# Attention and a low-rank mixer on one core: another order of the opening, up to batch 0's mixing

## The chip, the cores and the metric

The kernel runs on one core of a Trainium2 chip. A core has a matrix engine (TensorE, PE in the profile, with its weight loads as PEld), a vector engine (VectorE, DVE), a scalar engine (ScalarE, ACT), a general engine (GpSimd, POOL) and SyncE (SP), which only issues transfers. Each engine takes its instructions in order from its own queue and waits on semaphores for the others. Transfers between device memory and the on-chip memory (SBUF) are issued from SP's, ACT's or POOL's queue; those that change the type from float32 to float16 on the way are issued from POOL's. Matrix products are written to PSUM, which has eight banks here, and other engines read them from there.

The metric is the device time of one execution in microseconds (us), as a median over runs. The profile is of one execution on the same core.

## The reference

For 8 batches, 8 heads, 576 tokens and head size 64, it computes causal attention in which 16 extra "beacon" keys and values stand ahead of the batch's own, then a mixer on the attention's output `x` of 8 x 576 x 512:

```python
k_all = np.concatenate([beacon_k, k], axis=2)          # 16 + 576 keys
v_all = np.concatenate([beacon_v, v], axis=2)
scores = scale * np.matmul(q, k_all.transpose(0, 1, 3, 2))
scores = np.where(causal, -1000000000.0, scores)
a = softmax(scores)                                    # over the keys
x = np.matmul(a, v_all)                                # heads side by side: 512 columns
h = x.transpose(0, 2, 1) @ U @ V                       # U: 576 x 32, V: 32 x 576, along the tokens
u = x + h.transpose(0, 2, 1)
out = u + np.maximum(u @ w_ch1, 0.0) @ w_ch2           # 512 -> 2048 -> 512
```

## The kernel before

The work of the attention is cut into pairs of heads: pair `p` is heads `2c` and `2c+1` of batch `b`, with `b, c = divmod(p, 4)`, so pairs 0 to 3 are batch 0. For each pair q and k are brought into a tile `pr` (regroup, L240) and, for batch 0, a small head tile is cast beside it (L565). They are turned on PE (`qkT_units`, L248 and L250, into PSUM `tps`) and copied out as `qT` and `kT` (L251, L252; by ACT at L511). Scores are products at L304 into `sps`; one exponential per group of columns goes from there to `expt` (L310, ACT); the causal mask is a minimum with `bigmask`, which holds four blocks of the triangular `mask`, and with one small block of `mask` (L291, L293, DVE). The weighted sum of one head is 15 products at L328 into `po`; a column of ones in `vs` gives the divisor, and DVE divides (L336, L337) into `xb`.

When a batch has its eight heads in `xb`, it is mixed (`mix_units`): `head` multiplies with U (L368) and copies the result to `qts` (L374); two `part`s bring `xb` into `ups` by products with the identity (L387), add V times `qts` (L394), and copy to `uT` (L403 on DVE, L405 on ACT). V is spread over four groups of 32 partitions by a product with a selector `sel`, four identities side by side (`spread`, L157, copied at L160).

`uT` is then read by the two-layer network in blocks of 512 tokens (`mlp_units`). A block has 16 units of the hidden layer, dc 0 to 15, of four products each (L428, `gps`), each followed by a maximum with zero (L432, L434); then come units of the second layer (L445) and the output. w1 is loaded in four quarters of 512 columns by `emit_w1(i)` (L167): quarter `i` is what dc `4i` to `4i+3` read. w2 comes in two halves (`emit_w2`, L172).

The order of everything is written out by hand in `SCRIPT`, a string of steps. Under `tc.manual_schedule` each engine's queue has its instructions in the order in which the steps emit them. The steps that matter here:

- `GqV0`: regroup q of pair 0 on DVE (V; A is ACT, G is POOL). `TkA1`: turn k of pair 1, copied out by ACT.
- `Sa0:2`, `Sb0`: scores and exponentials of pair 0, groups 0 and 1, or 2 and 3; the number after the colon is how many idle products go first. `M0`: its masks. `A0.1`: the weighted sum of its second head.
- `I3`: three idle products of identity and identity, 512 columns each (`keep_warm`, L228), whose result is not used.
- `X0.0`, `X0.1`, `X0.2`: batch 0's mixing, head and two parts. After `X0.2` block 0's units join a list, and a step that is a number takes so many units from it; ahead of that the list is empty, and a number does nothing.
- `k1A`, `q1B`, `b1`, `v1A`: loads of batch 1, heads 0 to 3 (A) or 4 to 7 (B), by POOL; `b1` is its beacon keys. `w10` to `w13`, `w20`, `w21`: the quarters of w1 and the halves of w2, by POOL too.
- `u`: the small loads of U and V by SP (L141 to L146); `cV`: their casts (L150, L151); `eV`: the spread of V.

Batch 0's q and k are loaded as float32 by SP and ACT, ahead of the script. POOL's queue carries all the loads named above, and an issue there also waits until an earlier one of the same queue has landed: eight semaphores are used in turn (`semaphore=111` to `118` in the trace).

Of the kernel before, what the change touches and what calls it, by code (L numbers as in the profile page):

```python
# [17 lines left out]
P = 128  # L18
F16_MAX = 65504.0
# [8 lines left out]
def kernel(  # L28
# [75 lines left out]
    def pst(shape, dtype, name):  # L104
        return psum.tile(shape, dtype, tag="ps", name=name)


    ident = const.tile([P, P], F16, name="ident", tag="ident")
    make_identity(nc, ident)
    mask = const.tile([P, P], F16, name="mask", tag="mask")  # L110
    make_upper_triangular(nc, mask, val=F16_MAX, diag=True)
    bigmask = const.tile([P, 4, P], F16, name="bigmask", tag="bigmask")
    nc.vector.tensor_copy(out=bigmask[:, 0, 0 : P - Nb], in_=mask[:, Nb:P])
    nc.vector.memset(bigmask[:, 0, P - Nb : P], F16_MAX)
    for c in range(1, 4):
# [16 lines left out]
    def small_loads():  # L132

        f = utp.tile([P, NT * R + S], F32, name="small", tag="ut")
        uf, vf = f[:, 0 : NT * R].rearrange("p (j r) -> p j r", r=R), f[0:R, NT * R :]
        one = utp.tile([R, P + S], F16, name="one", tag="ut")
        sel, Vone = one[:, 0:P], one[:, P:]
        for cc in range(NCC):
            nc.vector.tensor_copy(out=sel[:, ts(cc, R)], in_=ident[0:R, 0:R])
        nc.vector.memset(uf[0:Nb, 0, :], 0.0)  # L140
        nc.sync.dma_start(out=uf[Nb:P, 0, :], in_=moe_U[0 : nq[0], :])  # L141
        nc.sync.dma_start(
            out=uf[:, 1 : NT - 1, :], in_=moe_U[q0[1] : QM, :].rearrange("(j p) r -> p j r", p=P)
        )
        nc.sync.dma_start(out=uf[:NL, NT - 1, :], in_=moe_U[QM:S, :])
        nc.sync.dma_start(out=vf, in_=moe_V)  # L146

        def cast(copy):
            for rr, jj in ((P, slice(0, NT - 1)), (NL, slice(NT - 1, NT))):
                copy(out=Usb[:rr, jj, :], in_=uf[:rr, jj, :])  # L150
            copy(out=Vone, in_=vf)  # L151
# [12 lines left out]
    def emit_w1(i):  # L164
        w1r = moe_w_ch1.rearrange("(cc p) f -> p cc f", p=P)
# [57 lines left out]
    def keep_warm(ps, n):  # L223


        w = ps.shape[-1] // P
        for _ in range(n):
            nc.tensor.matmul(  # L228
                ps[:, 0 : w * P].rearrange("p (a b) -> p a b", b=P), ident,
                ident.rearrange("p (a b) -> p a b", a=1).broadcast_to([P, w, P]),  # L230
                start=True, stop=True,
            )
# [386 lines left out]
    late = {}  # L619

    def step(t):
        name, arg = t[0], t[1:]
        if t.isdigit():
            fill(int(t))
        elif name == "I":
            keep_warm(pst([P, 512], F32, name="idle"), int(arg))
        elif name in "kqbv":
            b, hs = int(arg[0]), HALVES[arg[1:]]
            if name == "k":
                k_loads(b, L_of(b), hs)  # L630
# [36 lines left out]
        M2 A2.0 GqA5 A2.1 M3 GqA4 1 A3.0 w12 v1A A3.1 GkA5 eV w20 TqA5 GkA4 X0.0 1 X0.1 X0.2 TkA5 TqA4 TkA4 2  # L667
        k1B w21 2 v1B GqV6 Sb5 1 GqA7 Sa4 1 q2 2 Sb4 2 M4 4 A4.0 Sa5:0 2 GkA6 GkV7 M5 1 TqV6 1 A5.1 TkA6 b3
        A5.0 k2 1 A4.1 TkA7 Sa6:0 1 Sb6 TqV7 GqV8 2 GqV9 Sa7 2 M6 Sb7 b2 1 v2 A6.1 GkV9 GkV8 M7 1 TqV8 2 GkV10
        1 A6.0 GqA10 TqA10 q3 1 A7.1 A7.0 2 X1.0 X1.1 X1.2 TkA10 TqV9 TkV9 1 TkA8 1 Sa9 Sa8 3 Sb8 1 k3 GqA11 1  # L670
        v3 Sb9 M8 2 A8.1 A8.0 1 GkV12 1 GqV12 Sa10 1 M9 GkV11 R12 Sb10 1 M10 1 TkV11 1 A10.0 TqA11 4 GkA13
        A9.1 A9.0 Sa11 1 TkV12 GqV15 Sb11 1 k4 A10.1 2 GkA14 GqV13 1 TqA12 b5 Sa12 1 GqA14 M11 R13 R14 3 GkA15
        Sb12 1 A11.0 1 M12 A11.1 q4 TkA13 b4 TkV14 TqA13 Sa13 R15 A12.0 TqV14 1 TqV15 1 GkA16 3 Sb13 v4 1
        A12.1 M13 X2.0 2 Sb14 GqA18 A13.0 X2.1 TkV15 X2.2 A13.1 Sa14 k5 q5 GkA17 Sb15 GqA17 GqA16 R16 R17 1
# [134 lines left out]
```

## Time and profile before

| | us |
|---|---|
| median of 3 runs | 362.17 |
| lowest and highest of them | 361.27, 363.23 |
| the profiled execution, its own time | 360.71 |
| its span | 359.0 |
| busy in it: PE, ACT, DVE, POOL | 346.4, 207.0, 189.4, 82.8 |

A row of the timeline gives the start, the duration, the engine, the line, the operation, what it writes and reads, how many instructions are merged in it, and in brackets how long the engine had been idle and what ended that. "q" behind an engine's name means its queue, which issues a transfer; the time of an issue is not that of the transfer. A row of a stretch gives its length and then, per engine, busy time with the number of instructions, at its end PE's granted clock (1.00 is full speed), the share of the transfer engines and GB/s.

### The profile page before, as it was taken

The page shows a single profiled execution, that of the slowest core. Times are in us where ns is not written, and L with a number is a line of the kernel's source. Part 1 is how long each engine was busy: PE and PEld are TensorE (multiplying, and loading weights), DVE is VectorE, ACT ScalarE, POOL GpSimd, SP SyncE. Part 2 cuts the span into 40 slices and gives each one's busy share as a digit, 9 for nine tenths or more (in the row PEclk, how much of TensorE's full clock was granted, in tenths as well). Part 3 has the DMA queues.
Part 4 walks back from the last instruction along what each step waited for, and adds up shares of the span by engine and source line. Part 5 has one row for each costly group of instructions (what it writes and reads, how often), then busy time and mean ns, then how long its engine had stood idle before and what let it go on. Part 6 is the DMA issues. An engine that isn't in the chain of part 4 may idle for free.

```text
span 359.0 us, 7688 instructions
## 1 busy us (share of the span) xinstructions
PE 346.4 (96%) x3018; PEld 176.9 (49%) x3018; DVE 189.4 (53%) x528; ACT 207.0 (58%) x438; POOL 82.8 (23%) x119
## 2 busy tenths in 40 slices
PE   5989999999998999999999999999999999999995
PEld 2455478844545435454444544454544544444443
DVE  3884355546649455574757436774564446313311
ACT  3997866398579878658644954679335302401400
POOL 5993648601309006300620050000000000000000
PEclk9898999999999999999999999999999999999999
DMA  7999999992959969995999694663323123112111
GB/s 199 158 172 195 180 192 170 203 157 43 165 127 123 162 123 119 181 218 106 94 171 201 132 93 108 126 107 66 88 85 70 20 77 89 30 58 85 36 55 69
DMA packets 134396, 43.57 MB, mean 121 GB/s; under 512 B 106545, under 2 KB 130353, under 8 KB 134353
## 3 DMA queue, kind: packets, MB, share of 16 engines
q0 software_dynamic: 69008, 17.54, 51.4%
q1 hardware_dynamic: 64896, 25.17, 34.2%
q8 instruction: 25, 0.41, 0.5%
q10 hardware_dynamic: 448, 0.30, 0.3%
q14 instruction: 19, 0.15, 0.1%
HBM read 37.63 MB, written 9.44 MB: 131 GB/s over the span
## 4 chain that ended last, share of the span: by engine, by line
PE 86%; ACT 4%; DMA 4%; DVE 2%; POOL 1%; issue 1%; SPq 1%; ACTq 0%
PE cps L445 35%; PE gps L428 32%; PE po L328 7%; PE sps L304 7%; ACT expt L310 2%; DMA raw<-pr 2%; DMA vs<-in_v_dram 2%; PE ups L387 1%; PE ups L394 1%; PE tps L250 1%; POOL vs L190 1%; DMA stm<-in_k_dram 1%; PE qtp L368 1%; ACT pr L511 1%; ACT qT L511 1%
## 5 line engine op out<-in xcount | busy, mean ns | idle before, releaser
L310 ACT ACTIVATE expt<-sps 128x496 f16<-128x496 f32 (+2 forms) x256 | 110.7, 543 | 41.4 <-PE sps L304 38.6
L445 PE MATMUL cps<-w,gT 128*128 128x512 f16 (+1 forms) x656 | 134.2, 353 | 0.0
L428 PE MATMUL gps<-uT,w 128*128 128x512 f16 x576 | 132.8, 379 | 0.3 <-DVE xb L337 0.2
L432 ACT ACTIVATE gT<-gps 128x512 f16<-128x512 f32 x86 | 51.9, 621 | 70.0 <-PE gps L428 69.3
L445 PEld LDWEIGHTS <-gT 128*128 128x128 f16 x656 | 60.5, 98 | 57.6 <-issue 4.4
L428 PEld LDWEIGHTS <-w 128*128 128x128 f16 x576 | 53.0, 98 | 64.3 <-issue 3.5
L434 DVE TENSOR_SCALAR gT<-gps 128x512 f16<-128x512 f32 x58 | 39.9, 689 | 50.0 <-PE gps L428 48.0
L458 DVE TENSOR_TENSOR ob<-cps,ut 128x512 f32<-128x512 f32 (+1 forms) x33 | 22.2, 674 | 47.0 <-PE cps L445 46.6
L190 POOL DMA_DIRECT2D vs<-in_v_dram x50 | 40.7, 822 | 11.2 <-DMA w<-in_moe_w_ch_dram 5.6
L328 PEld LDWEIGHTS <-expt 128*128 128x128 f16 (+1 forms) x960 | 35.2, 98 | 13.8 <-DVE expt L291 2.2
L328 PE MATMUL po<-vs,expt 128*128 128x65 f16 (+1 forms) x960 | 38.4, 194 | 2.1 <-DVE expt L291 1.7
L304 PE MATMUL sps<-qT,kT 64*128 64x80 f16 (+4 forms) x384 | 35.9, 286 | 2.6 <-ACT kT L511 1.2
L337 DVE TENSOR_TENSOR xb<-po,rec 128x320 f16<-128x320 f32 x64 | 31.5, 491 | 2.2
L291 DVE TENSOR_TENSOR expt<-expt,bigmask 128x512 f16<-128x512 f16 x64 | 26.7, 417 | 8.8 <-ACT expt L310 8.8
L336 DVE RECIPROCAL rec<-po 128x5 f32<-128x5 f32 x64 | 12.0, 188 | 27.4 <-PE po L328 26.5
L304 PEld LDWEIGHTS <-kT 64*128 64x128 f16 x384 | 12.5, 95 | 25.5 <-issue 17.1
L180 POOL DMA_DIRECT2D vs<-in_beacon_v_dram x10 | 5.4, 544 | 66.8 <-PE po L328 66.8
L401 DVE TENSOR_TENSOR uT<-ups,xt 128x240 f16<-128x240 f32 (+3 forms) x40 | 15.5, 448 | 7.2 <-PE ups L394 7.2
L511 ACT ACTIVATE pr<-st 128x512 f16<-128x512 f16 x28 | 17.8, 666 | 0.0
L183 POOL DMA_DIRECT2D st<-in_k_dram x8 | 6.8, 852 | 39.4 <-ACT gT L432 21.3
L511 ACT ACTIVATE qT<-raw 128x512 f16<-128x512 f16 x10 | 11.0, 1105 | 4.6 <-DMA raw<-pr 4.6
L293 DVE TENSOR_TENSOR expt<-expt,mask 80x80 f16<-80x80 f16 x64 | 12.1, 189 | 0.0
(77 smaller groups left out, 168.6 us busy)
## 6 DMA issues: line engine op xcount, KB each, us to landing
out_dram<-ob SPq DMA_DIRECT2D x31, 256.0 KB, 2.3
st<-in_q_dram POOLq DMA_DIRECT2D x6, 512.0 KB, 9.9
st<-in_k_dram POOLq DMA_DIRECT2D x6, 512.0 KB, 8.9
vs<-in_v_dram POOLq DMA_DIRECT2D x18, 128.0 KB, 6.8
w<-in_moe_w_ch_dram POOLq DMA_DIRECT2D x4, 512.0 KB, 10.3
w<-in_moe_w_ch_dram POOLq DMA_DIRECT2D x2, 1024.0 KB, 11.1
out_dram<-ob SPq DMA_DIRECT2D x10, 128.0 KB, 5.5
stm<-in_k_dram SPq DMA_DIRECT2D x4, 256.0 KB, 3.3
```

The source lines that it names most:

```text
L190: nc.gpsimd.dma_start(out=dst[a : a + nq[j], j, :, :], in_=src[hs, ds(q0[j], nq[j]), :].rearrange("h p d -> p h d"))
L291: nc.vector.tensor_tensor(out=e4, in0=e4, in1=bigmask, op=ALU.min)
L304: nc.tensor.matmul(ps[g, i][:, ds(o, w)], kT[hp, c, ds(P * ch, P)], qT[hp, c, ds(qa, w)], start=True, stop=True,)
L310: nc.scalar.activation(out=ex[i][:, ds(PAD + SLOT * g, gw[g])], in_=ps[g, i][:, 0 : gw[g]], func=AF.Exp, scale=scale)
L328: nc.tensor.matmul(po[:, j, :], ex[0 : nk[c], ds(blk[(c, j)], P)], vs[0 : nk[c], ds(c * H * E + h * E, E)], start=(c == 0), stop=(c == j),)
L337: nc.vector.tensor_tensor(out=xb[:, h // 2, :, ds(D * (h % 2), D)], in0=po[:, :, 0:D], in1=r.broadcast_to([P, NT, D]), op=ALU.mult)
L428: nc.tensor.matmul(g[:, 0:n], w1[:, cc, ts(dc, P)], uT[:, cc, ds(ring(t0), n)], start=(cc == 0), stop=(cc == NCC - 1))
L432: nc.scalar.activation(out=gT["t"][:, dc, 0:n], in_=g[:, 0:n], func=AF.Relu)
L434: nc.vector.tensor_scalar_max(out=gT["t"][:, dc, 0:n], in0=g[:, 0:n], scalar1=0.0)
L445: nc.tensor.matmul(ps[:m, :], gT["t"][:, dc, ds(P * i, m)], w2[:, dc, ds(cs, w)], start=(dc == 0), stop=turned and dc == NDC - 1, skip_gro ...
L458: nc.vector.tensor_tensor(out=ob[:m, :], in0=ps[:m, :], in1=gT["u"][:m, i, ds(cs, w)], op=ALU.add)
L511: nc.scalar.activation(out=out, in_=in_, func=AF.Copy)
```

## The change

Only what is issued before and during batch 0's mixing is touched. `bigmask` is filled by a step of its own (`B`, after `Sb0`) rather than at the start, with its memset first. The four copies that make the selector move from `u` to a step `s`, after `Sb2`. U and V are cast by POOL (`cG` for `cV`). Pairs 0 to 3 are regrouped and turned in another order and partly on other engines (`TkA0 TqV0` come first, `Sa0` ahead of `Sb0`; `TkA2` and `TkV3` for `TkV2` and `TkA3`; `GqV3` for `GqA3`), pair 5's k is regrouped on DVE (`GkV5`), the last pair's scores come as `Sa3`, `Sb3`, and `TqA4` and `TqA5` stand ahead of the mixing. Idle products: `Sa0:1`, `Sa1:3`, `Sa2:2`, `Sa3:3`, and `I2`, `I2`, `I3` between and after the last weighted sums; before there were `I3`, `Sa0:2`, `Sa2:2` and `Sa3:2`, with `I10` at the start in both. The loads on POOL come as `b1 v0A v0B q1A k1A w13`, the casts, `w10 q1B w12 w11 w20 k1B v1A w21 v1B`. From `TkA5 2 v1B` on the script is as it was.

```diff
@@ -110,10 +110,13 @@
     bigmask = const.tile([P, 4, P], F16, name="bigmask", tag="bigmask")
-    nc.vector.tensor_copy(out=bigmask[:, 0, 0 : P - Nb], in_=mask[:, Nb:P])
-    nc.vector.memset(bigmask[:, 0, P - Nb : P], F16_MAX)
-    for c in range(1, 4):
-        nc.vector.tensor_copy(out=bigmask[:, c, :], in_=mask)
+
+    def fill_bigmask():
+        nc.vector.memset(bigmask[:, 0, P - Nb : P], F16_MAX)
+        nc.vector.tensor_copy(out=bigmask[:, 0, 0 : P - Nb], in_=mask[:, Nb:P])
+        for c in range(1, 4):
+            nc.vector.tensor_copy(out=bigmask[:, c, :], in_=mask)
+
...
@@ -135,8 +138,6 @@
-        for cc in range(NCC):
-            nc.vector.tensor_copy(out=sel[:, ts(cc, R)], in_=ident[0:R, 0:R])
...
+
+        def select():
+            for cc in range(NCC):
+                nc.vector.tensor_copy(out=sel[:, ts(cc, R)], in_=ident[0:R, 0:R])
...
-        return cast, spread
+        return cast, spread, select
...
-            late["c"], late["e"] = small_loads()
+            late["c"], late["e"], late["s"] = small_loads()
+        elif name == "B":
+            fill_bigmask()
+        elif name == "s":
+            late[name]()
...
-        I10 GqV0 1 GkG0 GqV1 GkG1 v0A TqA0 TkA1 GkV2 TkA0 GqV2 v0B GkV3 Sb0 u 1 Sa0:2 TqV1 TkA3 GqA3 I3 Sb1
-        k1A M0 TkV2 TqV3 TqV2 cV Sa1:0 M1 A0.1 q1A A0.0 Sb2 q1B b1 Sa2:2 w10 1 w13 A1.0 A1.1 Sb3 Sa3:2 w11 1
-        M2 A2.0 GqA5 A2.1 M3 GqA4 1 A3.0 w12 v1A A3.1 GkA5 eV w20 TqA5 GkA4 X0.0 1 X0.1 X0.2 TkA5 TqA4 TkA4 2
-        k1B w21 2 v1B GqV6 Sb5 1 GqA7 Sa4 1 q2 2 Sb4 2 M4 4 A4.0 Sa5:0 2 GkA6 GkV7 M5 1 TqV6 1 A5.1 TkA6 b3
+        1 GqV0 I10 GkG0 TkA0 b1 GkG1 v0A GqV1 v0B TqV0 GkV2 Sa0:1 u q1A GqV2 TkA1 TkA2 TqV1 GkV3 Sb0 B GqV3 M0
+        TkV3 Sb1 TqV2 Sa1:3 k1A 2 w13 1 TqV3 A0.1 M1 cG A0.0 1 Sb2 w10 s Sa2:2 A1.1 A1.0 M2 GkV5 Sa3:3 I2 A2.1
+        Sb3 GqA4 1 q1B GqA5 M3 eA A2.0 I2 A3.0 A3.1 GkA4 TqA4 w12 TqA5 I3 X0.0 X0.1 w11 w20 X0.2 TkA4 2 k1B
+        v1A w21 TkA5 2 v1B GqV6 Sb5 1 GqA7 Sa4 1 q2 2 Sb4 2 M4 4 A4.0 Sa5:0 2 GkA6 GkV7 M5 1 TqV6 1 A5.1 TkA6
...
```

More of the change, by code (lines that the diff above doesn't have):

```diff
@@ L664 @@
     SCRIPT = """
-        I10 GqV0 1 GkG0 GqV1 GkG1 v0A TqA0 TkA1 GkV2 TkA0 GqV2 v0B GkV3 Sb0 u 1 Sa0:2 TqV1 TkA3 GqA3 I3 Sb1
-        k1A M0 TkV2 TqV3 TqV2 cV Sa1:0 M1 A0.1 q1A A0.0 Sb2 q1B b1 Sa2:2 w10 1 w13 A1.0 A1.1 Sb3 Sa3:2 w11 1
-        M2 A2.0 GqA5 A2.1 M3 GqA4 1 A3.0 w12 v1A A3.1 GkA5 eV w20 TqA5 GkA4 X0.0 1 X0.1 X0.2 TkA5 TqA4 TkA4 2
-        k1B w21 2 v1B GqV6 Sb5 1 GqA7 Sa4 1 q2 2 Sb4 2 M4 4 A4.0 Sa5:0 2 GkA6 GkV7 M5 1 TqV6 1 A5.1 TkA6 b3
[L669 to L674, printed above, removed]
+        1 GqV0 I10 GkG0 TkA0 b1 GkG1 v0A GqV1 v0B TqV0 GkV2 Sa0:1 u q1A GqV2 TkA1 TkA2 TqV1 GkV3 Sb0 B GqV3 M0
+        TkV3 Sb1 TqV2 Sa1:3 k1A 2 w13 1 TqV3 A0.1 M1 cG A0.0 1 Sb2 w10 s Sa2:2 A1.1 A1.0 M2 GkV5 Sa3:3 I2 A2.1
+        Sb3 GqA4 1 q1B GqA5 M3 eA A2.0 I2 A3.0 A3.1 GkA4 TqA4 w12 TqA5 I3 X0.0 X0.1 w11 w20 X0.2 TkA4 2 k1B
+        v1A w21 TkA5 2 v1B GqV6 Sb5 1 GqA7 Sa4 1 q2 2 Sb4 2 M4 4 A4.0 Sa5:0 2 GkA6 GkV7 M5 1 TqV6 1 A5.1 TkA6
+        b3 A5.0 k2 1 A4.1 TkA7 Sa6:0 1 Sb6 TqV7 GqV8 2 GqV9 Sa7 2 M6 Sb7 b2 1 v2 A6.1 GkV9 GkV8 M7 1 TqV8 2
+        GkV10 1 A6.0 GqA10 TqA10 q3 1 A7.1 A7.0 2 X1.0 X1.1 X1.2 TkA10 TqV9 TkV9 1 TkA8 1 Sa9 Sa8 3 Sb8 1 k3
+        GqA11 1 v3 Sb9 M8 2 A8.1 A8.0 1 GkV12 1 GqV12 Sa10 1 M9 GkV11 R12 Sb10 1 M10 1 TkV11 1 A10.0 TqA11 4
+        GkA13 A9.1 A9.0 Sa11 1 TkV12 GqV15 Sb11 1 k4 A10.1 2 GkA14 GqV13 1 TqA12 b5 Sa12 1 GqA14 M11 R13 R14 3
+        GkA15 Sb12 1 A11.0 1 M12 A11.1 q4 TkA13 b4 TkV14 TqA13 Sa13 R15 A12.0 TqV14 1 TqV15 1 GkA16 3 Sb13 v4
+        1 A12.1 M13 X2.0 2 Sb14 GqA18 A13.0 X2.1 TkV15 X2.2 A13.1 Sa14 k5 q5 GkA17 Sb15 GqA17 GqA16 R16 R17 1
         M14 1 Sa15 x12 3 TkV16 A14.1 TqA16 1 A14.0 k6 4 M15 GkA18 x13 1 R18 TkA17 1 TqV17 Sb16 2 Sa16 A15.1
```

## The prediction

> **What bounds the kernel now.** I read the page's head first, then the work of TensorE (PE) in stretches of about 3.4 us, then PE's timeline around batch 0's mixing, then GpSimd's (POOL) timeline with the landings of its transfers.
>
> ```profile
> span 359.0 us, 7688 instructions
> PE 346.4 (96%) x3018; PEld 176.9 (49%) x3018; DVE 189.4 (53%) x528; ACT 207.0 (58%) x438; POOL 82.8 (23%) x119
> ```
>
> PE is busy 346.4 of 359.0 us. What is left to win lies in the opening, and whatever delays the opening is paid in full at the end. The next rows give, per stretch, each engine's busy time, then PE's clock, the share of DMA and GB/s.
>
> ```profile
> 12.00:15.40 3.40, 2.69 (x35) 1.62 (x35) 2.98 (x16) 3.40 (x10) 2.87 (x5) 0.99 1.92 164
> 15.50:18.90 3.40, 3.25 (x48) 1.66 (x45) 3.31 (x12) 3.40 (x10) 3.28 (x6) 1.00 0.98 70
> 18.90:22.30 3.40, 3.15 (x65) 2.15 (x65) 2.86 (x11) 3.40 (x11) 3.40 (x6) 1.00 1.52 178
> 22.30:25.70 3.40, 2.01 (x48) 1.48 (x44) 3.03 (x11) 3.40 (x8) 3.01 (x6) 1.00 1.44 190
> 25.70:29.20 3.50, 3.50 (x49) 2.70 (x49) 2.23 (x6) 2.00 (x6) 2.14 (x3) 0.51 1.23 207
> 29.20:32.60 3.40, 3.40 (x34) 1.98 (x32) 1.61 (x3) 2.91 (x9) 0.65 (x1) 1.00 1.24 205
> ```
>
> Three things are to be seen. ACT is full (3.40 of 3.40) from 12 to 25.7 us: the exponentials set when the weighted sums can end. After the one stretch in which PE was busy for only 2.01 of 3.40 us, the clock stands at 0.51 for the next stretch; after 2.69 of 3.40 it stays at 1.00. And the transfers run at 70 GB/s from 15.5 to 18.9, then at 178 to 207: from 18.9 us on, what lands is set by bytes.
>
> ```profile
> 24.09 1.35 PE L328 MATMUL po<-vs,expt 128*128 128x65 f16 x30 [1.31 <-DVE expt L291]
> 26.32 0.72 PE L368 MATMUL qtp<-xb,Usb 128*32 128x128 f16 x20
> 29.34 0.32 PE L394 MATMUL ups<-Vsb,qts 32*128 32x336 f16 x4
> 29.59 0.21 PE L248 MATMUL tps<-ident,hd 80*128 80x80 f16 x1
> 29.86 0.20 PE L248 MATMUL tps<-ident,hd 80*128 80x80 f16 x1
> 30.39 3.62 PE L428 MATMUL gps<-uT,w 128*128 128x512 f16 x16
> 33.94 0.48 PE L304 MATMUL sps<-qT,kT 64*128 64x336 f16 x8
> 34.35 1.04 PE L428 MATMUL gps<-uT,w 128*128 128x512 f16 x4
> ...
> 68.94 0.47 PE L368 MATMUL qtp<-xb,Usb 128*32 128x128 f16 x20
> 71.04 0.21 PE L248 MATMUL tps<-ident,hd 80*128 80x80 f16 x1
> ```
>
> Batch 0's mixing runs from 26.32 to 29.59, 3.27 us, in the slow stretch; batch 1's, the same products at full clock, from 68.94 to 71.04, 2.10 us. Keeping the clock is so worth 1.17 us at most. Then come the hidden layer's products of block 0: units dc 0 to 3 (16 matmuls) at 30.39, the scores Sb5 at 33.94, and dc 4 at 34.35. Units dc 4 to 7 read the second quarter of w1 (emit_w1(1), w11 in the script). PE takes its instructions in order, so where w11 is late, all of PE is late.
>
> ```profile
> 16.34 0.75 POOL L183 DMA_DIRECT2D st<-in_k_dram  x1
> 17.68 0.75 POOL L183 DMA_DIRECT2D st<-in_q_dram  x1
> 19.80 0.66 POOL L177 DMA_DIRECT2D hd<-in_q_dram  x1
> 20.44 0.55 POOL L180 DMA_DIRECT2D hd<-in_beacon_k_dram  x1
> 20.97 3.01 POOL L167 DMA_DIRECT2D w<-in_moe_w_ch_dram  x4
> ...
> 27.76 0.74 POOL L190 DMA_DIRECT2D vs<-in_v_dram  x1 [0.67 <-DMA w<-in_moe_w_ch_dram]
> 31.46 0.65 POOL L190 DMA_DIRECT2D vs<-in_v_dram  x1 [2.95 <-DMA w<-in_moe_w_ch_dram]
> 33.96 1.16 POOL L172 DMA_DIRECT2D w<-in_moe_w_ch_dram  x1 [1.85 <-DMA w<-in_moe_w_ch_dram]
> 36.51 0.75 POOL L183 DMA_DIRECT2D st<-in_k_dram  x1 [1.39 <-DMA w<-in_moe_w_ch_dram]
> ...
> st<-in_q_dram POOLq DMA_DIRECT2D x1, 256.0 KB, 5.2
> w<-in_moe_w_ch_dram POOLq DMA_DIRECT2D x1, 512.0 KB, 13.0
> hd<-in_beacon_k_dram POOLq DMA_DIRECT2D x1, 16.0 KB, 4.6
> ```
>
> The last three rows are issues taken alone: q1A's main part (17.68), the fourth quarter of w1 (23.2) and beacon_k of batch 1 (20.44), with us to landing. The fourth quarter lands at 23.2 + 13.0 = 36.2; POOL, held by the quarters in turn, goes on 0.3 us later, at 36.51. By that distance the earlier restarts put the others at 27.5, 31.2 and 33.7. The order now is w10, w13, w11, w12, so w11 lands at 33.7, 0.65 us before dc 4 wants it.
>
> **The change, part by part.**
>
> *The order of POOL's loads.* From 16.34 on, POOL's queue held k1A, q1A, q1B, b1, w10, w13, w11, w12. Now b1 goes ahead of all, and the rest is q1A, k1A, w13, the casts, w10, q1B, w12, w11, w20. The same pieces less b1 are wanted before w11 is complete, and w11 is now the last of them. Their sum is 36.2 less b1's 16 KB, 0.1 us at 178 GB/s: w11 lands at about 36.1. I find nothing that starts the line sooner: q1A's issue takes the place of k1A's at 16.34, behind the same twelve v transfers. The bounds: if the 70 GB/s of 15.5 to 18.9 became 178, 3.4 x 108 = 367 KB would be ahead, at 205 GB/s 1.8 us, and w11 at 34.3; if the casts leave the queue empty for 1 us, 37.1. I take 36.1, since the old order shows that hole too. v1A goes behind w20 and k1B; its pieces end where k1B's did less b1, and A4.0, its first reader, moves back by as much as dc 4, so I add nothing. q1B behind w10, and w21 behind v1A, have readers later than dc 4.
>
> *b1 ahead of GkG1.* POOL's idle time hides its issue:
>
> ```profile
> 4.07 0.61 POOL L240 CAST pr<-stm 128x512 f16<-128x512 f32 x1 [1.89 <-DMA stm<-in_k_dram]
> 5.28 0.29 POOL L565 CAST hd<-sth 80x128 f16<-80x128 f32 x1 [0.60 <-DMA sth<-in_beacon_k_dram]
> 6.11 0.62 POOL L240 CAST pr<-stm 128x512 f16<-128x512 f32 x1 [0.54 <-DMA stm<-in_k_dram]
> ```
>
> It takes 0.55 us, and POOL waits 0.54 before 6.11. Without that cover all v transfers would start 0.55 us later.
>
> *U and V cast on POOL.* Three casts leave DVE and come between w13's and w10's issue, at about 19.8.
>
> ```profile
> 16.52 0.55 DVE L150 CAST Usb<-small 128x128 f16<-128x128 f32 x2
> 16.73 0.62 DVE L151 CAST one<-small 32x576 f16<-32x576 f32 x1
> ```
>
> On DVE they fill 16.52 to 17.35, 0.83 us. On POOL I price them from its rows by elements per partition: V 0.61 x 576/512 = 0.7, U 0.3 and 0.2, 1.2 us in all; at worst double, 2.4. So w10 is issued at 21.0 to 22.2. The queue ahead then holds k1A until 17.68 + 5.2 = 22.9 and w13 for 512 KB / 205 = 2.5 us more, until 25.4: covered. The Trainium skill, SBUF — State Buffer, "Who interferes with whom", has a GpSimd operation and a DVE copy in a two-port mode shut each other out of a shared port for a whole instruction. No run here shows such a pair; by that rule, which speaks against this move, the casts would tend to their upper price.
>
> *Block copies of mask (0.5 us), selector (0.4), the casts gone from DVE.* These are waits of DVE for data or lie beside ACT's full stretch. I take 0; -0.5 to +0.5, all ahead of dc 4. New on DVE is GkV5 between the masks M2 and M3: it waits for k1A, 22.9 by the row above, with A2.1's division and M3 queued behind it.
>
> *Transposes and copies of pairs 0 to 3.*
>
> ```profile
> 7.49 1.34 ACT L511 ACTIVATE kT<-tps 128x80 f16<-128x80 f16 x4 [0.76 <-PE tps L250]
> 9.51 3.63 ACT L310 ACTIVATE expt<-sps 128x496 f16<-128x496 f32 x8 [0.68 <-PE sps L304]
> 13.01 0.76 ACT L511 ACTIVATE kT<-tps 128x80 f16<-128x80 f16 x2
> 13.76 0.63 ACT L511 ACTIVATE pr<-stm 128x512 f16<-128x512 f32 x1
> ...
> 12.34 0.81 PE L228 MATMUL idle<-ident 128*128 128x512 f16 x3
> ```
>
> Between the first and the last exponential ACT did one pair of copies (0.76) and a cast (0.63 and its small one); now it does the two pairs TkA1 and TkA2 (1.34). That is even. Sa1 now may wait for a bank of PSUM that TkV3's copy frees, and TkV3 stands behind M0 on DVE: 0 to 1 us. With GkV5's wait I let the mixing begin 0.5 us later, at 26.8 (26.3 to 27.8).
>
> *Idle products.* Seven more than now, at 0.22 us (the pitch in 12.34 to 13.08), 1.5 us, put where PE had 0.25 + 1.39 us idle from 18.9 to 25.7. If they hold the clock, mixing takes 2.10: it ends at 28.9. dc 0 followed the last mixing product by 30.39 - 29.34 = 1.05 us, for the copies to uT; so dc 0 starts near 29.7, a gain of 0.7.
>
> *Then w11.* From dc 0, PE has 3.55 us of dc 0 to 3 (30.39 to 33.94), one transpose set more than now (0.27, 29.59 to 29.86) and Sb5 (0.41): dc 4 is wanted at 33.9 and gets w11 at 36.1, starting at 36.15. PE stands for about 2.2 us. Against 34.35 that is +1.8, whatever the mixing gained; by the bounds 0 to +2.8. A standstill of 2.2 us leaves a stretch with 1.2 of 3.4 busy, less than the 2.01 that was followed by half clock: one stretch at half costs up to 1.7 us. I take 1.5, since the standstill can fall across two stretches. A gap of 1.31 us (the row at 24.09) already came before the half clock. The Trainium skill, TensorE: Matmul & The Clock Gate, "HAM oscillation — how this bites in real kernels", sums its rule up as "no PE-idle gaps >~3.4µs"; by it the clock would hold after 2.2 us and the cost stay +1.8, and the trace does not agree.
>
> **The sum.** The profiled execution took 360.71 us (span 359.0 and 1.7 around it), below all three runs shown (361.27 to 363.23, median 362.17). 360.71 + 1.8 + 1.5 = 364.0; the median stands 1.46 above, which gives 365.5. Part of what makes the other runs longer must lie ahead of dc 4, where the wait for w11 swallows it; I take a third of 1.46 off: 365.0.
>
> **The rivals.**
> 1. *The wait, but full clock.* Where the standstill falls half into one stretch and half into the next, neither may be idle enough: 365.0 - 1.5 = 363.5. For it: after 2.69 of 3.40 the clock held. Against it: after 2.01 it did not. The rule of the Trainium skill quoted above would give this time as well.
> 2. *The hole in the loads closes.* w11 at 34.3: dc 4 is where it was, 362.2. The regular pace after 18.9 speaks for it; the same issue times speak against.
> 3. *Faster: the clock decides, not w11.* The idle products hold the clock through the mixing. With no delay before it, the mixing ends at 26.3 + 2.1 = 28.4, dc 0 starts at 29.2 (at best) and dc 4 at 33.4, 0.9 before 34.35; I add 1.1 for slow stretches that make the median run 1.46 longer than the profiled one and that the products would end too: 362.2 - 0.9 - 1.1 = 360.2. It decides only where w11 lands by 33.4, 2.7 us before my sum; the fourth quarter's 13.0 us speaks against it.
> 4. *POOL's casts hold the loads back.* w11 at 37.1 and a full slow stretch: 365.0 + 1.0 + 0.2 = 366.2, with w10 near dc 0 as well.
>
> **How the numbers follow.** Forecast 50%, rival 1 15%, rival 2 15%, rival 3 10%, rival 4 10%. Half a per cent of 362.17, 1.8 us, is about what a measurement of this kernel can tell: faster below 360.4, slower above 364.0. Rival 3 gives faster 0.10; rival 2 and most of rival 1 give the same, 0.28; the forecast, rival 4 and the rest of rival 1 give slower, 0.62. The range leaves out rival 3 and the far end of rival 4: 362.0 to 366.8; the forecast alone has 364.0 to 366.5.
>
> **What would show it.** Right: PE's first wait after the mixing stands before a product at L428 and is released by a transfer into w, about 2 us long, ending near 36; a stretch of about 3.4 us at half clock follows; the mixing itself takes near 2.1 us; the fourth w1 load on POOL lands last. Wrong: dc 4 runs on without a wait, or w11 lands before 34; the wait is there but the clock stays at 1.00 (rival 1); POOL shows casts far over 1.2 us and a gap in the transfers before w10 (rival 4).

## The result, and the profile after

| | before | after |
|---|---|---|
| median of the runs taken together, us (22 each) | 361.2 | 363.37 |
| lowest and highest, us | 359.08, 363.23 | 361.58, 367.48 |
| ratio after to before, 95% interval | | 1.0057 (1.0036 to 1.0078) |
| the profiled execution: its own time, its span, us | 360.71, 359.0 | 362.54, 360.9 |

By the ratio the change makes the kernel slower by about 2.05 us (0.57% of 361.2); the two medians stand 2.17 apart. The prediction said 365.0 where the median was 362.17, a ratio of 1.0078.

The head of the page after:

```profile
span 360.9 us, 7695 instructions
PE 348.6 (97%) x3025; PEld 177.7 (49%) x3025; DVE 189.6 (53%) x528; ACT 205.7 (57%) x435; POOL 84.2 (23%) x122
```

PE has its seven more products, the idle ones. Next, PE's timeline of the kernel after, from batch 0's mixing to the first product of the second layer (L450, L445 before); the line numbers are 5 higher than before.

```profile
28.51 0.68 PE L373 MATMUL qtp<-xb,Usb 128*32 128x128 f16 x20
...
30.83 0.21 PE L253 MATMUL tps<-ident,hd 80*128 80x80 f16 x1
...
31.42 1.89 PE L433 MATMUL gps<-uT,w 128*128 128x512 f16 x8 [0.16 <-ACT uT L410]
...
36.53 1.04 PE L433 MATMUL gps<-uT,w 128*128 128x512 f16 x4 [0.82 <-DMA w<-in_moe_w_ch_dram]
...
46.31 0.62 PE L333 MATMUL po<-vs,expt 128*128 128x65 f16 x15
46.86 0.58 PE L309 MATMUL sps<-qT,kT 64*128 64x496 f16 x4
...
49.11 1.04 PE L450 MATMUL cps<-w,gT 128*128 128x256 f16 x8
```

The same last product in the kernel before, in PE's timeline:

```profile
46.93 1.04 PE L445 MATMUL cps<-w,gT 128*128 128x256 f16 x8
```

| | before | after | later by |
|---|---|---|---|
| mixing begins | 26.32 | 28.51 | 2.19 |
| mixing ends (its length) | 29.59 (3.27) | 30.83 (2.32) | 1.24 |
| dc 0 begins | 30.39 | 31.42 | 1.03 |
| dc 4 begins | 34.35 | 36.53 | 2.18 |
| first product of the second layer | 46.93 | 49.11 | 2.18 |
| from there to the end of the span | 312.1 | 311.8 | |

All that the change costs is there when dc 4 begins, and dc 4 begins when a transfer into w has landed: the predicted wait, in the predicted place. It is 0.82 us long, not 2.2, because the mixing itself began 2.19 us later than before. The table sets one execution of each kernel beside one of the other, and single executions differ: experiments 5 and 7, which the runs can't tell from before, have dc 4 at 35.41 and 35.46. Why the mixing began so late is seen in PE's stretches, ACT's timeline and the two rows of PE that belong to it, all of the kernel after. The columns of the stretches are those of the prediction.

```profile
8.40:11.80 3.40, 2.81 (x23) 1.70 (x24) 2.15 (x8) 2.20 (x6) 3.40 (x6) 0.51 1.06 246
11.80:15.20 3.40, 2.63 (x27) 1.56 (x24) 3.37 (x16) 3.35 (x10) 3.40 (x5) 0.50 1.90 162
15.20:18.60 3.40, 3.40 (x30) 1.74 (x29) 1.73 (x5) 2.35 (x6) 3.40 (x6) 0.50 1.33 88
...
28.80:32.20 3.40, 3.24 (x54) 2.17 (x54) 1.94 (x5) 2.70 (x9) 1.97 (x3) 1.00 1.37 201
...
35.60:39.00 3.40, 2.58 (x17) 0.92 (x14) 0.63 (x2) 2.93 (x7) 0.74 (x1) 1.00 1.45 198
39.00:42.40 3.40, 3.40 (x23) 1.43 (x21) 0.69 (x1) 3.40 (x9) 0.34 (x1) 1.00 1.70 183
```

```profile
16.86 1.96 ACT L315 ACTIVATE expt<-sps 128x496 f16<-128x496 f32 x4 [1.05 <-PE sps L309]
19.58 2.01 ACT L315 ACTIVATE expt<-sps 128x496 f16<-128x496 f32 x5 [0.76 <-ACT expt L315]
```

```profile
14.82 1.49 PE L233 MATMUL sps<-ident 128*128 128x512 f16 x3
16.24 0.98 PE L309 MATMUL sps<-qT,kT 64*128 64x496 f16 x4
```

The mixing runs at full clock now, but the clock is at 0.50 from 8.4 to 18.6, where before it was so from 8.68 to 12.09 and from 25.74 to 29.16 (by the trace's clock). ACT, which was full from 12 us on before, has lost 1.05 us to the scores Sa1: the three idle products ahead of them (14.82) take 1.49 us at that clock. It has lost 0.76 us at 19.58 more, ahead of pair 2's exponentials: their scores (Sb2) stand behind pair 0's weighted sums in PE's queue, and PE has no idle time from 15.20 to 18.60, at half clock, so here ACT waits for PE. (The buffer of `expt` that these exponentials reuse was free a little sooner: pair 0's weighted sums had ended at 19.17, the first of the scores at 19.50.) The copy of the spread of V is on ACT too now (`eA` for `eV`, which the list of the change leaves out): two copies, 0.80 us from 27.07.

Last, POOL's timeline of the kernel after:

```profile
6.44 0.66 POOL L185 DMA_DIRECT2D hd<-in_beacon_k_dram  x1 [0.31 <-issue]
7.10 0.63 POOL L245 CAST pr<-stm 128x512 f16<-128x512 f32 x1
...
8.12 0.51 POOL L185 DMA_DIRECT2D vs<-in_beacon_v_dram  x1
...
16.76 0.78 POOL L188 DMA_DIRECT2D st<-in_q_dram  x1
...
20.21 0.51 POOL L155 CAST Usb<-small 128x128 f16<-128x128 f32 x2
20.59 0.72 POOL L156 CAST one<-small 32x576 f16<-32x576 f32 x1
21.20 0.79 POOL L172 DMA_DIRECT2D w<-in_moe_w_ch_dram  x1
...
34.23 0.74 POOL L195 DMA_DIRECT2D vs<-in_v_dram  x1 [2.04 <-DMA w<-in_moe_w_ch_dram]
36.77 0.74 POOL L195 DMA_DIRECT2D vs<-in_v_dram  x1 [1.79 <-DMA w<-in_moe_w_ch_dram]
42.06 0.65 POOL L195 DMA_DIRECT2D vs<-in_v_dram  x1 [4.56 <-DMA w<-in_moe_w_ch_dram]
```

The next cast begins where b1 (6.44) ends, and the first issue for v is at 8.12; the line of loads behind the v transfers starts at 16.76, 0.42 later than in this execution of the kernel before (16.34). The casts take 1.1 us, from 20.21 to 21.31. The last three rows are pieces of v1A, each held until a load of w has landed: w12, w11 and then the first half of w2.

### The profile page after: what moved, and what is told of

Read it like the earlier page. It is cut to its first block, busy times and chain, and to the rows that moved or that the text cites. A ratio compares the mean times of both kernels' runs of the same rounds, so it can differ in the third digit from the quotient of the medians.

```text
span 360.9 us, 7695 instructions
## 1 busy us (share of the span) xinstructions
PE 348.6 (97%) x3025; PEld 177.7 (49%) x3025; DVE 189.6 (53%) x528; ACT 205.7 (57%) x435; POOL 84.2 (23%) x122
## 4 chain that ended last, share of the span: by engine, by line
PE 81%; DMA 6%; POOL 5%; ACT 3%; DVE 2%; issue 1%; SPq 0%; ACTq 0%; POOLq 0%
PE cps L450 35%; PE gps L433 31%; PE po L333 7%; PE sps L309 6%; DMA w<-in_moe_w_ch_dram 3%; POOL vs L195 2%; DMA raw<-pr 2%; ACT expt L315 1%; DMA sth<-in_beacon_k_dram 1%; PE ups L399 1%; PE tps L255 1%; DVE xb L342 1%; PE qtp L373 1%; ACT pr L516 1%; POOL w L172 1%
## 5 line engine op out<-in xcount | busy, mean ns | idle before, releaser
L450 PE MATMUL cps<-w,gT 128*128 128x512 f16 (+1 forms) x656 | 134.2, 353 | 0.0
L450 PEld LDWEIGHTS <-gT 128*128 128x128 f16 x656 | 60.5, 98 | 57.5 <-issue 4.4
L463 DVE TENSOR_TENSOR ob<-cps,ut 128x512 f32<-128x512 f32 (+1 forms) x33 | 22.2, 674 | 47.2 <-PE cps L450 46.8
```

What stands on the lines that cost most here:

```text
L450: nc.tensor.matmul(ps[:m, :], gT["t"][:, dc, ds(P * i, m)], w2[:, dc, ds(cs, w)], start=(dc == 0), stop=turned and dc == NDC - 1, skip_gro ...
L463: nc.vector.tensor_tensor(out=ob[:m, :], in0=ps[:m, :], in1=gT["u"][:m, i, ds(cs, w)], op=ALU.add)
```

## The experiments

The theory (called L in the expectations) is that the order of the loads makes the loss: w11 is last of the quarters, so that dc 4 is late, and the v1A pieces stand behind w20. The rivals: the opening's new order of work itself (called O), the half clock (C), b1, and the casts or small moves. Each kernel is timed beside the kernel before; a step of the script is shown without the steps around it.

**1. The quarters of w1 in the order of their readers, the rest as after.**

```diff
-... k1A 2 w13 1 ... Sb2 w10 s ... X0.1 w11 w20 X0.2
+... k1A 2 w10 1 ... Sb2 w11 s ... X0.1 w13 w20 X0.2
```

> The changed kernel with the quarters of w1 issued in the order in which they are read (w10, w11, w12, w13 in the places of w13, w10, w12, w11). Theory L (late quarter): in the changed kernel's profile dc 4 starts at 36.53, 0.05 us after w11 lands, while PE was done with the scores before it at 35.7. Without the wait dc 4 starts at 35.7, 0.8 us sooner; if L were all of the loss, the ratio to the kernel before falls from 1.0057 to 1.000. Theory O (the opening itself is later: the mixing starts at 28.51 instead of 26.32, at 2.3 us instead of 3.3 long): 1.3 us stay, ratio 1.0035. If the late quarter costs nothing in most runs, 1.0057 stays.

Measured: 363.04 us, ratio 1.0042 (1.0021 to 1.0062). The wait at dc 4 is gone, and yet the kernel is not level with before. PE's timeline of this kernel, then POOL's:

```profile
34.62 1.04 PE L433 MATMUL gps<-uT,w 128*128 128x512 f16 x4
...
44.44 0.52 PE L333 MATMUL po<-vs,expt 128*128 128x65 f16 x5
45.15 0.28 PE L333 MATMUL po<-vs,expt 128*128 128x65 f16 x4 [0.19 <-DMA vs<-in_v_dram]
45.65 0.34 PE L333 MATMUL po<-vs,expt 128*128 128x65 f16 x6 [0.22 <-DMA vs<-in_v_dram]
45.92 0.58 PE L309 MATMUL sps<-qT,kT 64*128 64x496 f16 x4
...
48.17 1.04 PE L450 MATMUL cps<-w,gT 128*128 128x256 f16 x8
```

```profile
42.45 0.65 POOL L195 DMA_DIRECT2D vs<-in_v_dram  x1 [4.59 <-DMA w<-in_moe_w_ch_dram]
```

dc 4 starts at 34.62, 0.27 later than in the kernel before. But the weighted sum A4.0 now waits for pieces of v1A. From its start to the next scores there are 45.92 - 44.44 = 1.48 us; in the kernel after they are 0.55 (46.31 to 46.86). So 0.93 us are lost again. The last piece was issued at 42.45, since POOL had been held 4.59 us by the first half of w2, which now goes first. Of the 1.91 us won at dc 4, 0.94 are left at the first product of the second layer (48.17 against 49.11). The runs can't tell this kernel from the one after.

**2. The kernel before with w11 last of the quarters, nothing else.**

```diff
-... Sa3:2 w11 1 ... A3.0 w12 v1A ...
+... Sa3:2 w12 1 ... A3.0 w11 v1A ...
```

> The kernel before with w11 and w12 exchanged in POOL's queue and nothing else: w11 then lands at 36.2 in place of 33.7, and the opening is untouched. Theory L: dc 4 starts near 36.3 instead of 34.35, with PE standing for 1.9 us: ratio 1.005, and up to 1.010 if a stretch at half clock follows the standstill. If the wait is absorbed by slack later in the kernel: 1.000. Theory O says nothing against L here; it only says that this is not what happens in the changed kernel, where PE came late as well.

Measured: 364.23 us, 1.0064 (1.0035 to 1.0094). One swap of two loads costs as much as the whole change. PE's timeline and its stretches:

```profile
29.20 3.62 PE L428 MATMUL gps<-uT,w 128*128 128x512 f16 x16
...
36.37 1.27 PE L428 MATMUL gps<-uT,w 128*128 128x512 f16 x4 [3.15 <-DMA w<-in_moe_w_ch_dram]
```

```profile
33.60:37.00 3.40, 0.63 (x3) 0.31 (x4) 0.14 (x1) 1.15 (x4) 1.55 (x2) 1.00 1.85 163
37.00:40.40 3.40, 3.40 (x11) 0.87 (x10) 0.00 (x0) 2.72 (x6) 3.17 (x5) 0.51 1.45 184
40.40:43.80 3.40, 3.40 (x22) 1.44 (x21) 0.69 (x1) 2.29 (x6) 1.68 (x3) 0.99 1.48 196
```

This is the forecast's picture in full: dc 4 starts at 36.37 (I had 36.15 for the change), PE stands 3.15 us, and a stretch at half clock follows, in which 11 products are done where the next has 22. Here the mixing was early, as I had assumed for the change. In this profile the first product of the second layer is 3.61 us later than before (50.54 for 46.93); the ratio stands for 2.3 us, so not every execution can have paid that much.

**3. Without the idle products ahead of Sa0 and Sa1.**

```diff
-... Sa0:1 u ... Sa1:3 k1A
+... Sa0:0 u ... Sa1:0 k1A
```

> The changed kernel without the one idle product of Sa0 and the three of Sa1. Theory O: in the changed kernel's profile these three ran from 14.82 to 16.24 at half clock, and ACT stood 1.05 us for the scores behind them; without them the mixing starts about 1 us sooner. Theory L: dc 4 then only waits longer for w11, which still lands at 36.5, so the ratio stays at 1.0057 (PE's standstill grows from 0.8 to about 1.8 us, and a stretch at half clock may follow, 1.010). O without L: 1.003.

Measured: 362.55 us, 1.0039 (1.0012 to 1.0065), not to be told from the kernel after. Half clock stood from 8.4 to 18.6 in this profile as well, the mixing began at 28.94 and dc 4 at 37.40, after 1.36 us of waiting for w. ACT did gain: it no longer stood for Sa1, and pair 2's exponentials began 0.60 us sooner (18.98 for 19.58). But then DVE stood for k1A, which the copy for pair 5 (`GkV5`) reads, and PE for a division behind that copy. DVE's and PE's timelines:

```profile
25.34 0.29 DVE L245 COPY pr<-st 128x512 f16<-128x512 f16 x1 [2.41 <-DMA st<-in_k_dram]
```

```profile
26.31 0.60 PE L233 MATMUL idle<-ident 128*128 128x512 f16 x2 [1.43 <-DVE xb L342]
```

So the early idle products are not what lowers the clock, and what they cost ACT is not what costs the kernel its time: two loads, k1A and then w11, come later still.

**4. b1 back behind q1B.**

```diff
-... TkA0 b1 GkG1 ... q1B GqA5
+... TkA0 GkG1 ... q1B b1 GqA5
```

> The changed kernel with b1 back behind q1B, as in the order before. In the changed kernel's profile b1's issue (0.66 us, and 0.31 idle ahead of it) stood in front of the second regroup, and v0A's issue began at 8.12 instead of 6.90. Theory L: all loads start up to 0.9 us sooner, w11 lands at 35.6 to 36.2 instead of 36.5, ratio 1.003 to 1.005. Theory O: nothing else in the opening waits for these loads except the first weighted sum; the mixing stays near 28.5 and the ratio at 1.0057, or up to 0.5 us less.

Measured: 363.03 us, 1.0055 (1.0028 to 1.0083): no gain. The mixing began at 27.45, but now the beacon keys of batch 1 were late for the transpose ahead of dc 0, and dc 4 waited for w11 all the same. PE's timeline:

```profile
31.54 0.21 PE L253 MATMUL tps<-ident,hd 80*128 80x80 f16 x1 [1.81 <-DMA hd<-in_beacon_k_dram]
...
36.45 0.82 PE L433 MATMUL gps<-uT,w 128*128 128x512 f16 x3 [0.35 <-DMA w<-in_moe_w_ch_dram]
```

PE loses 1.81 us at one place and stands 0.47 less at the other (0.35 for 0.82), and dc 4 is where it was (36.45 for 36.53): what comes ahead of w11's landing doesn't show. The first issue for v came at 7.30 here instead of 8.12, but the line of loads began at 16.81, no sooner than with b1 early (16.76): POOL had stood 0.60 and 0.36 us for v transfers to land. So the later start of that line isn't b1's doing.

**5. All of POOL's loads in the order before, the rest as after.**

```diff
-TkA0 b1 GkG1 ... u q1A ... Sa1:3 k1A 2 w13 1 ... Sb2 w10 s ... GqA4 1 q1B ... w12 TqA5 ... X0.1 w11 w20 ... k1B v1A w21
+TkA0 GkG1 ... u ... Sa1:3 k1A q1A 2 q1B b1 1 ... Sb2 w10 w13 s ... GqA4 1 w11 ... w12 v1A TqA5 ... X0.1 w20 ... k1B w21
```

> The changed kernel with POOL's loads in the order before (k1A q1A q1B b1 w10 w13 w11 w12 v1A w20 k1B w21 v1B, the casts still on POOL ahead of w10); all else as changed. It takes away the late w11 (36.5), the late v1A (in the kernel with the quarters in order, A4.0 waited for its pieces and the second layer came about 1 us late), the late k1A that held DVE for 1.4 to 2.4 us in three of the profiles, and b1 ahead of the v loads. Theory L (the order of the loads is the whole loss): 1.000, or 0.998 if the idle products then keep the clock in the mixing. Theory O (the new order of pairs 0 to 3 itself leaves ACT idle for about 1 us before pair 2's exponentials): the mixing starts at 27.0 or later and the ratio is 1.002 to 1.004.

Measured: 362.23 us, 1.0011 (0.998 to 1.0041). No difference from before that the runs can tell is left. dc 4 started at 35.41 without a wait in its profile, the first product of the second layer at 47.99. Both are 1.06 us later than in the profile of the kernel before, so this one profile doesn't show the loss gone; the runs do, as far as their interval goes.

**6. The kernel before with six idle products ahead of M3.**

```diff
-... A2.1 M3 ...
+... A2.1 I6 M3 ...
```

> The kernel before with six idle products between the weighted sums A2.1 and A3.0 and nothing else, where its profile has PE idle from 22.8 to 24.1 and a half clock from 25.7 to 29.2. Theory C (the half clock in the mixing costs what the two mixings differ by): no half clock in the mixing, 2.1 to 2.4 us of mixing instead of 3.3, dc 4 then bound by w11 at 33.7, so at most 0.6 us sooner: ratio 0.997 to 0.999 (only some executions have the half clock there: in the profile with w11 and w12 exchanged the mixing ran at full clock without them). Rival: they delay the last weighted sums by what they take past the wait, ratio 1.000 to 1.002.

Measured: 360.73 us, 0.9977 (0.9951 to 1.0003). PE's timeline:

```profile
26.39 0.61 PE L368 MATMUL qtp<-xb,Usb 128*32 128x128 f16 x20
28.66 0.21 PE L248 MATMUL tps<-ident,hd 80*128 80x80 f16 x1
...
34.30 1.04 PE L428 MATMUL gps<-uT,w 128*128 128x512 f16 x4 [0.81 <-DMA w<-in_moe_w_ch_dram]
```

The clock was 1.00 throughout the opening, the mixing took 2.27 us instead of 3.27, and then dc 4 waited 0.81 us for w11 and began at 34.30, where it began before (34.35). In this profile a faster mixing buys nothing, even in the order before; the runs leave between 0 and 0.5% of gain open.

**7. The kernel before with b1 early.**

```diff
-... GkG0 GqV1 ... q1B b1 Sa2:2
+... GkG0 b1 GqV1 ... q1B Sa2:2
```

> The kernel before with b1 issued behind GkG0, as in the changed kernel, and nothing else. The prediction took its issue as hidden by 0.54 us of idle time: ratio 1.000. The changed kernel's profile speaks for a cost: b1 (0.66 us) stands before the second regroup, the v loads begin 0.6 us later, pair 0's weighted sums wait for them and pair 2's exponentials for the weighted sums: mixing 0.6 us later, ratio 1.001 to 1.002.

Measured: 360.74 us, 0.9986 (0.9959 to 1.0013). POOL's timeline:

```profile
6.38 0.67 POOL L180 DMA_DIRECT2D hd<-in_beacon_k_dram  x1 [0.32 <-issue]
...
8.08 0.97 POOL L180 DMA_DIRECT2D vs<-in_beacon_v_dram  x1
```

The first v issue comes at 8.08, as in the kernel after (8.12), and not at 6.90 as in the kernel before, but the runs show no cost. In this profile the mixing began 0.75 us later than before (27.07) and dc 4 1.11 later (35.46, without a wait for w); that is one execution, and the interval leaves room for 0.13%, or 0.5 us.

**8. The kernel before with the mask's copies, the selector and the casts moved as in the change.**

```diff
+    def fill_bigmask(): ...
+    def select(): ...
-... Sb0 u 1 ... TqV2 cV Sa1:0 ... Sb2 q1B b1 Sa2:2
+... Sb0 u B 1 ... TqV2 Sa1:0 ... Sb2 s q1B b1 cG Sa2:2
```

> The kernel before with only the three small moves: mask's block copies behind Sb0, the selector behind Sb2, U's and V's casts on POOL just ahead of w10. The prediction took 0 for DVE and found the casts hidden behind the loads queued ahead: ratio 1.000 (0.999 to 1.001). If POOL's casts (1.1 us in the changed kernel's profile) hold the loads back, w11 lands up to 1.1 us later than 33.7, past the 34.35 at which dc 4 wants it: ratio up to 1.002.

Measured: 361.2 us, 1.0009 (0.9983 to 1.0035): nothing, as costed.

**9 and 10. The kernel before with w11 ahead of w13, with and without the idle products of experiment 6.** Can the early mixing be used, if w11 lands earlier?

```diff
-... Sa2:2 w10 1 w13 A1.0 ... Sa3:2 w11 1 ... A2.1 M3
+... Sa2:2 w10 1 w11 A1.0 ... Sa3:2 w13 1 ... A2.1 I6 M3
```

Experiment 10 leaves out the `I6`.

> The kernel before with the six idle products between A2.1 and A3.0 and with w11 ahead of w13 in POOL's queue (w10 w11 w13 w12). With the idle products alone the clock held through the mixing and dc 4 then waited 0.8 us for w11 (34.3, w11 landed at 34.25). Theory L: with w11 at about 31.5 that wait goes too, dc 4 starts at 33.4, and the ratio is 0.995 to 0.997. If the wait was made up elsewhere: 0.998, as with the idle products alone.

> The kernel before with w11 ahead of w13 alone. In its profile dc 4 did not wait (34.35, w11 at 33.68), but only because the mixing ran at half clock; in executions where it does not, dc 4 can wait up to 0.7 us. Theory L: ratio 0.999 to 1.000, and no wait for w at dc 4 in any case. Rival: w13 later makes dc 12 wait, above 1.000 (w13 then lands at 33.7, dc 12 is wanted near 42, so I do not expect it).

Measured: 360.88 us, 1.0002 (0.9969 to 1.0035), and 361.0 us, 0.999 (0.9959 to 1.0021). dc 4 began at 34.34 and 34.43 without a wait for w. The profile of 9 had its half clock from 14.49 to 17.9. No version that is faster than the kernel before has been shown.

**11. The change with w1 in order and v1A ahead of w20.** Experiment 1 left a second late load; this one takes it away.

```diff
-... k1A 2 w13 1 ... Sb2 w10 s ... X0.1 w11 w20 X0.2 TkA4 2 k1B v1A w21
+... k1A 2 w10 1 ... Sb2 w11 s ... X0.1 w13 v1A w20 X0.2 TkA4 2 k1B w21
```

> The changed kernel with the quarters of w1 in order and v1A ahead of w20; b1 first, q1A ahead of k1A and everything else as changed. With the quarters alone in order (1.0042) A4.0 had waited for v1A and the second layer came 1 us late. Theory L: 0.7 to 1 us less than that, 1.0015 to 1.002; with all loads back it was 1.0011. Theory O, that the rest of 1.0042 is the opening's own order: 1.004 stays.

Measured: 361.2 us, 0.9989 (0.996 to 1.0018). PE's timeline:

```profile
27.71 0.57 PE L373 MATMUL qtp<-xb,Usb 128*32 128x128 f16 x20
29.92 0.21 PE L253 MATMUL tps<-ident,hd 80*128 80x80 f16 x1
30.52 1.89 PE L433 MATMUL gps<-uT,w 128*128 128x512 f16 x8 [0.16 <-ACT uT L410]
...
34.74 1.04 PE L433 MATMUL gps<-uT,w 128*128 128x512 f16 x4
...
47.32 1.04 PE L450 MATMUL cps<-w,gT 128*128 128x256 f16 x8
```

Two moves of loads take the change's whole loss away, with everything else of it in place. The opening's own order (O) so costs nothing that can be measured: its mixing begins 1.4 us later than before (27.71 for 26.32), takes 1.1 less (2.21 for 3.27), and dc 0 is level (30.52 for 30.39). The interval lies just below that of experiment 1 (up to 1.0018 there, from 1.0021 here), so the late v1A is told apart too. Its size in the runs, 0.5%, is more than the 0.93 us that the profile of experiment 1 shows; why, is not settled. The profile of experiment 1 also has 1.26 us of a wait near 130 us that is described at the end, and for which one execution says little.

**12. The change without the idle products after pair 2's and 3's scores.**

```diff
-... Sa3:3 I2 A2.1 ... A2.0 I2 A3.0 ... TqA5 I3 X0.0
+... Sa3:3 A2.1 ... A2.0 A3.0 ... TqA5 X0.0
```

> The changed kernel without I2, I2 and I3 at the last weighted sums; loads as changed. Theory C: PE then stands in those waits, a half clock follows in part of the executions and the mixing takes up to 1.2 us more; but dc 4 waits for w11 in any case (36.5), so most of it only takes the place of that wait: ratio 1.005 to 1.008. Rival: the idle products themselves delay the mixing, and without them it is sooner: dc 4 still waits for w11, so no lower than 1.005.

Measured: 363.37 us, 1.0051 (1.0022 to 1.0079), level with the kernel after. PE's timeline:

```profile
36.43 1.04 PE L433 MATMUL gps<-uT,w 128*128 128x512 f16 x4 [1.13 <-DMA w<-in_moe_w_ch_dram]
```

dc 0 is 0.41 us earlier (31.01 for 31.42). Of that 0.31 goes into a longer wait for w11 (1.13 for 0.82), and dc 4 is 0.10 earlier, as w11 is.

## Why the prediction was right, and where its steps were not

**The bound and the place: right.** w11 is the last piece wanted and dc 4 waits for it; I had 36.15 for its start, it was 36.53. The 0.38 between them is about the later start of the line of loads (16.76 for 16.34), which differs by as much between executions: with the order before it lies at 15.89 in experiment 10 and at 16.66 in experiment 6. Experiment 2 makes the loss with that one swap, experiments 5 and 11 take it away by the loads alone, and experiments 3, 4 and 12, which change what comes ahead, leave it. (Experiment 1 shows that w11's place alone is not the whole: v1A's is the rest.) One of my reasons needs care: "v1A goes behind w20 ... I add nothing" holds only while w11 delays A4.0 as well. That was cover, not absence of cost; experiment 1 takes the cover off and finds 0.93 us.

**The sum, term by term.** 360.71 + 1.8 + 1.5 + 1.0 = 365.0 was the forecast; 360.71 + 1.83 + 0 + 0.83 = 363.37 is what came. The first term, the wait, is the difference of the two profiled executions' own times (362.54 - 360.71). The last is the distance from the profiled execution to the median. The term that was mis-sized is "one stretch at half costs up to 1.7 us. I take 1.5": no half clock follows the wait in the profile after; the stretch with the wait still had 2.62 us of PE busy. Rival 1's time, 363.5, is so the nearest, though not for its reason: the standstill did not fall across two stretches, it was only 0.82 us long. By the signs that the prediction gave, a wait with the clock at 1.00 behind it is rival 1, which had 15%, and not the forecast, which had 50%. The median is within the range (362.0 to 366.8), and below what I gave for the forecast alone (364.0 to 366.5). It is also below 364.0, the line above which I called the kernel slower; that it is slower rests on the ratio, since the median of before came out lower than the one I had. Of the 1.6 us between 365.0 and 363.37, 1.5 is the half clock that didn't come. That the first term held although the mixing began 1.7 us later than I had it is no merit of the sum: w11 hid it.

**Why the standstill was short: the step that failed is "I let the mixing begin 0.5 us later, at 26.8 (26.3 to 27.8)".** It began at 28.51. I had counted ACT's copies and casts as even and given a waiting Sa1 0 to 1 us. In the profile ACT stood 1.05 us for Sa1, behind idle products at half clock, and 0.76 us for the scores behind pair 0's weighted sums, at half clock as well, 1.81 of the 2.19 us. How the rest divides is not told apart. The half clock itself, three stretches of it early on, was not in the sum at all. `GkV5`'s wait for k1A, which I had named, is absent from the profile after (the copy runs at 23.74 without one), because ACT was later still. Where ACT was earlier it came: 1.41, 1.50 and 1.72 us in experiments 1, 4 and 11, with 0.57 to 0.74 us of PE standing behind it, near the 0.5 I gave; their mixing begins at 27.45 to 27.71, 1.1 to 1.4 later than before. The late start cost nothing in the end, since w11 hid it: in experiment 12 dc 0 is 0.41 us earlier, in experiment 3 the mixing is 0.43 later, and dc 4 goes with w11 in both. Without a late w11 (experiment 11) it is paid back by the mixing at full clock.

**The idle products: worth nothing, and their mechanism not shown.** With them the clock holds through the mixing (2.32 us; I had 2.10), and the gain of 0.95 us ends in the wait for w11. That they are what holds it is not shown: it held without them too, in experiment 12, and in experiments 2 and 8 in the order before. Seven of them take 1.7 us, at 0.25 each (12.34 to 13.08 for three); the 0.22 and 1.5 of the prediction are not in that row. Experiment 6 has the same wait in the order before. So rival 3, faster by the clock, falls on the point that I gave for it: w11 doesn't land by 33.4 (34.30 in experiment 6). And where w11 did land earlier, experiment 9, the runs show no gain either.

**b1: "POOL's idle time hides its issue" was wrong in the profile.** Its issue took 0.66 us with only 0.31 idle ahead of it, and the cast behind it began at 7.10; in experiment 4, the same kernel without it, at 6.50. As the prediction had it for that case, the transfers for v started later. No price of that shows in the runs, though (experiment 7, 0.9986), and in experiment 4 the line of loads behind v began no sooner without it.

**The casts: right.** 1.1 us for 1.2, w10 issued at 21.20 (21.0 to 22.2), covered; rival 4 falls. Rival 2, the hole in the loads closing, falls with w11's 36.5. The masks, the selector and the casts together measure 1.0009 in experiment 8, where I took 0.

**The offset.** With 22 runs the median of before is 361.2, not 362.17: the profiled execution stood 0.5 below it, not 1.46. Three runs were too few for a term of 1.0 in a sum of 4.3.

## What to carry to other kernels

Loads that share a queue landed one after another here (quarters of w1 about 2.5 us apart), so they are put in the order in which their first readers come, and moving one means asking what every load behind it now delays: the swap of two quarters of a weight matrix cost as much here as the whole change. Work that is won ahead of a wait for a transfer is worth nothing until that transfer lands earlier, and a cost found to be "hidden" is hidden only behind the thing that is late now; take that away and it shows. Where two profiled executions are compared, it is done up to a place behind the change, since stretches at a lower clock and waits elsewhere differ between executions by as much as the change is worth.

## What the runs showed of the hardware that was not expected

**Stretches at half clock come in nearly every trace and mostly cost little.** In the traces they last 3.41 us or a multiple of it (8.43 to 18.67 in the kernel after), and begin somewhere else in each: 8.68 in the kernel before, 14.19 in experiment 1, 10.53 in experiment 5. In that of experiment 6 there is none. Each run also gives its mean granted clock, which one such stretch lowers by 0.0047 (3.41 x 0.5 / 361). The 22 runs of the kernel after have 0.9897 on average, 2.2 stretches or 7.4 us; the 104 runs of the kernel before that were taken beside the experiments have 0.9924, 1.6 stretches or 5.5 us. Within one kernel's runs, a run is longer by 0.13 us (standard error 0.02) for each us at half clock. If that is taken as a price, the lower clock explains 1.9 x 0.13 = 0.25 of the 2.05 us; it is a correlation, and no run sets the clock by itself. A likely reading, not tested, is that a stretch costs its full 1.7 us only where PE is what everything waits for, as from 15.20 to 18.60 in the kernel after, and that in the opening it mostly is not.

**What brings half clock on.** In each trace the stretches lie on a grid of 3.41 us: 8.68 and 25.74 in the kernel before are five steps apart, 9.73 and 37.03 in experiment 2 eight. The length of a gap doesn't decide. PE stood 1.31 us ahead of the last weighted sums in the kernel before and in experiments 2, 7, 8 and 10; half clock followed in the kernel before, 7 and 10, and not in 2 and 8, nor after the 1.81 us of experiment 4. What goes with it is how long PE was busy in the step of that grid just ahead. Counted over the thirteen traces with such a stretch, half clock followed all 14 steps with up to 1.80 us busy, 4 of the 15 with 1.86 to 2.17, and none with more. Out of half clock, steps with 3.18 us busy and more were followed by full clock, those with 2.85 and less were not: so the kernel after, busy for 2.85, 2.65 and 3.41 us, stayed there for three steps. The Trainium skill, TensorE: Matmul & The Clock Gate, "HAM oscillation — how this bites in real kernels", has "no PE-idle gaps >~3.4µs"; gaps of 1.31 and 3.15 us had half clock behind them, so for this kernel the measurement decides against the figure as a safe limit.

**DVE's copies beside POOL's cast.** The four selector copies in the timeline of the kernel before, and the same copies and V's cast in that of the kernel after:

```profile
11.93 0.39 DVE L139 COPY one<-ident 32x32 f16<-32x32 f16 x4
```

```profile
20.59 0.72 POOL L156 CAST one<-small 32x576 f16<-32x576 f32 x1
20.84 0.74 DVE L151 COPY one<-ident 32x32 f16<-32x32 f16 x4
```

Begun in the middle of the cast, the copies took 0.74 us instead of 0.39 and ended 0.27 behind it, and the cast kept its price. In experiment 12, begun with the first of the three casts, they took 1.14 us and ended with the last. That fits the page cited in the prediction, the Trainium skill's SBUF — State Buffer, "Who interferes with whom", by which one of the two shuts the other out; but the copies also took 0.54 us in experiment 8 without a cast beside them, so it is not shown that this is the cause. Experiment 8 shows that the time of the kernel doesn't depend on it.

**A wait far from the change.** Near 130 us PE waits before a hidden unit, at the end of a chain through a transposing transfer (`raw<-pr`), between 0.0 and 1.9 us, whatever the kernel: 0.21 in the kernel before, about 0 in the one after and in experiments 7, 11 and 12, 1.26 in experiment 1, 1.75 in experiment 6 and 1.92 in experiment 5. The last two are level with before in the runs, so it is most likely one execution's chance, as large as the effect under study.
